# Eight pairs of hidden columns in two groups of seven products, with first writers of the output found at build time

## The chip, the cores and the metric

The kernel runs on one core of one Trainium2 chip. A core has five engines that run side by side and wait for one another through semaphores: TensorE (PE in the profile, its weight loads PEld), VectorE (DVE), ScalarE (ACT), GpSimd (POOL) and SyncE (SP), the last used here to issue DMAs. Matmuls write PSUM, of which the kernel has eight banks; everything else lies in SBUF or in DRAM. The metric is the device time of one execution in microseconds; before the change it is 1256.85 us, the median of three runs (1254.98 to 1257.09).

## What is computed

The reference sums the input, a long-convolution block and a feed-forward block (S = 2048 rows, D = 1024, F = 3584, float32):

```python
x = A_q
xn = _layernorm(x, axis=-1)
return x + _A_ref(xn, A_k, A_v, A_shift_k, A_ssm_k, A_ssm_D) + _B_ref(xn, B_w1, B_w2)
```

`_A_ref` filters `k` with four taps, multiplies by `v`, convolves each channel over the whole sequence (by FFT) with `ssm_k`, adds `kv * ssm_D`, and multiplies by `q`, here the normalised input. `_B_ref` is `silu(xn @ w1) @ w2`. The two matrix products are called GEMM1 and GEMM2 below.

## The kernel before

**Precision.** Every float32 operand of a large matmul is split into two float16 parts, and three matmuls (high x high, high x low, low x high) replace one. `split` makes the parts: ScalarE writes the high half (`a_act`, L360), VectorE the low half (`v_stt`, L352). Each split thus costs one ScalarE and one VectorE instruction over the same elements.

**Seven products.** GEMM1 takes the hidden columns in pairs of 128-column blocks (14 pairs, `NP`) and the rows in halves, and computes each 2 x 2 block product with seven products (P1 to P7, `PRODUCTS`) in place of eight. The price is sums and differences of blocks (S1 to S4, T1 to T4) ahead of the products. `units` runs the pairs for the first two row blocks (sp = 0) and then for the others (sp = 1); `evacuate` reads the PSUM banks, and `silu` follows.

**What becomes of the hidden activations.** For a plain pair `blocks` makes one 1024-wide split for each of the four row blocks and stores it in DRAM (`hs`). For a pair in `PAIRS` (8 to 11) `quad` makes, for each sp, three 1024-wide splits, one 512-wide split and four 512-wide sums, and stores seven tiles (`hsf`): the left operands of the seven products in GEMM2.

**GEMM2.** It runs in two halves of the output columns (h = 0 is the right half, `columns`), each half over 16 rows of 128 (t) and, for the plain pairs, five chunks of four hidden blocks (`NC` = 5), 12 matmuls a chunk (`steps2`, L1074 to L1076). Then `units2` runs pairs 8 to 11: eight tiles of seven products, each product 12 matmuls, each tile giving four 128 x 512 pieces of output (`evacuate2`). The W2 side is prepared by `norms_w2`: plain chunks by two 1024-wide splits each, the seven products by 28 narrow splits and 16 sums, in eight SBUF places that are handed on from GEMM1 (`W2PLACE`, `FPLACE`).

**The convolution** runs behind this in eight groups of 128 channels: `gate` (taps, times v), `signal_parts` (splits), `stage1` (matmuls with a DFT matrix), `to_spec` (PSUM to SBUF, ScalarE and VectorE), `forward`, `product` and `inverse` (butterflies and products on VectorE), `result_parts` (splits), `stage1_inv` (matmuls back), `gated` (times the normalised input, and out). A first transform may start only when the group before has finished its product, and its results may be written only once `result_parts` has taken the old ones (`taken`). Its PSUM tiles come from two banks (`ps_r`); `stage1_inv` has two others (`py_r`). During the plain part of GEMM2 both may also use a spare bank of the feed-forward ring `ff` (`spare`).

**Output.** Several contributions to each element of the output are summed in DRAM: one writer stores plainly (`L`, a DMA of the SP queue), the others accumulate (`G`, a DMA issued by GpSimd). Before the change it is fixed who writes first: `result` for h = 0, and the convolution's groups 0 to 3 for h = 1; all others wait for the flags `row` and `conv row` and accumulate. The last tile of GEMM2 waits for all of the convolution (`conv out`), reads back its piece (`hf<-out`), adds it and stores plainly.

**Order.** The program is written by generators, streams with a bias in microseconds. `Order.run` keeps a time for each engine and takes next the operation with the least start minus bias; of those that are ready at one time the largest bias goes first. Each engine then runs its instructions in the order so found. Quads have 0.1, evacuations 0.06, W2 0.05, the convolution 0.04 down to 0.02.

Of the kernel before, what the change touches and what calls it, by code (L numbers as in the profile page):

```python
# [53 lines left out]
PAIRS = (8, 9, 10, 11)  # L54
UNITS = [[*range(2, NP)], [NP - 1, 0, 1, *range(2, NP - 1)]]
NQ = len(PAIRS)
# [244 lines left out]
def h3_ffn_kernel(ctx, tc, x, kp, vs, fs, shift, dskip, w1, w2, cfwd, cinv, out):  # L301
# [77 lines left out]
    hsf = [{p[0]: dram.tile([4, P, NQ, 2, P], F16, name=f"hsf{p[0]}{b}") for p in PRODUCTS.values()} for b in range(2)]  # L379
# [449 lines left out]
    def quad(i, sp):  # L829

        def factors(names, hf, toks=()):
            n = len(names)
            yield hts.ready if n == 1 else hts.pairs
            ht, ttok = (hts.tile if n == 1 else hts.pair)([P, 4 * n, 2, P], F16, n)
            yield from split(ht[:, :, 0], ht[:, :, 1], hf, wsc[:, i, 2:3], toks)
            for f, name in enumerate(names):
                yield L(hsf[sp][name][:, :, PAIRS.index(i)].rearrange("q p h s -> p q (h s)"),
                        ht[:, 4 * f:4 * f + 4].rearrange("p q h s -> p q (h s)"))
# [12 lines left out]
        yield v_tt(z, x, z, SUB)  # L851
        add(factors(("S3", "S1"), flat[1], (ltok,)), 0.1)
        yield v_tt(x, v, x, SUB)
        ltok.set()
        yield v_tt(y, y, x, SUB)
        add(factors(("S2", "S4"), flat[0], (utok, flag["quads", sp])), 0.1)

    for sp in range(2):
        flag["quads", sp] = Token(NQ)

# [170 lines left out]
    def feed_forward():  # L1031
        first = [xo[0]["A11"], xo[0]["A12"]]
        r = [flag["rows", t] for t in range(4)]
        yield from plain_unit(0, 0, first, (r, r), 2)
        yield from plain_unit(1, 0, first, ((), ()))
        yield flag["x", 0, "A22"]
        lower = [second["A21"], xo[0]["A22"]]
        r = [(flag["x", 0, "A21"],), (flag["x", 0, "A22"],)]
        yield from plain_unit(0, 1, lower, r, free=True)
        yield from plain_unit(1, 1, lower, r, free=True)  # L1040
        second["tok"].set()
        flag["room", 0].set()
        yield from units()
        flag["gemm1"].set()
        for h in range(2):
            for ts in TOGETHER[h]:
                pos = {}
                for c in range(NC):
                    for t in ts:
                        if c == 0:  # L1050
                            yield ff.ready
                            pos[t] = ff.tile([P, W])
                        yield flag["h", h, t, c]
                        hx, htok = flag["h", h, t, c].what
                        yield flag["w2", h, c]
                        wc, wtok = w2c[h, c]
                        yield from steps2(pos[t][0], hx, wc, c == 0, c == NC - 1)
                        htok.set()
                        if t == NT - 1:
                            wtok.set()  # L1060
                        if c == NC - 1:
                            add(result(h, t, *pos[t]), EB)
        flag["last part"].set()
        yield from units2()


    TOGETHER = ([range(2)] + [(t,) for t in range(2, NT)],
                [(t,) for t in range(NT - 3)] + [range(NT - 3, NT)])

    def steps2(po, hx, wc, first, last, more=False):  # L1070
        for n in range(4):
            def mm(n=n):
# [3 lines left out]
                nc.tensor.matmul(po, hx[:, n, 1, :], wc[:, n, 0, :], start=False, stop=last and n == 3, **kw)  # L1076
# [15 lines left out]
    def units2():  # L1092

        def product2(n, u, o, first=False):
            yield flag["h2", u, n]
            hx, htok = flag["h2", u, n].what
            yield flag["w2f", n]
            wc, wtok = w2f[n]
            yield from steps2(o, hx, wc, first, True, not first)
# [7 lines left out]
        for u in range(len(tiles2)):  # L1107
# [3 lines left out]
            add(evacuate2(u, one, c, made, seen), EB)  # L1111
# [20 lines left out]

    def at(u, r, h):

        sp, q = tiles2[u]
        t = 4 * (2 * sp + r) + q
        return orr[t // T2, t % T2, :, h * W:(h + 1) * W]

    def evacuate2(u, one, c, made, seen):

        last = u == len(tiles2) - 1

        def copied(src, tok, to):
# [4 lines left out]
            yield G(to, o)  # L1148
# [12 lines left out]
        add(copied(*one, at(u, 0, 0)), EB)  # L1161
# [7 lines left out]
        yield G(at(u, 1, 1), d)  # L1169
# [9 lines left out]
        add(copied(two, k2, at(u, 0, 1)), EB)  # L1179
# [3 lines left out]
        yield L(at(u, 1, 0), a) if last else G(at(u, 1, 0), a)  # L1183
# [3 lines left out]
    for n in range(NT):  # L1187
        flag["conv row", n] = Token(NG // 2)

    def columns(h):  # L1190

        return slice((1 - h) * W, (2 - h) * W)

    def result(h, t, po, tok):
# [4 lines left out]
        to = orr[t // T2, t % T2, :, columns(h)]  # L1199
        if h == 0:  # L1200
            yield L(to, o)
            flag["row", t].set()
        else:
            yield flag["conv row", t]
            yield G(to, o)
        otok.set()

    def load_h():
        yield flag["factors"]
        for h in range(2):  # L1210
            for c, t in [(c, t) for ts in TOGETHER[h] for c in range(NC) for t in ts]:
# [4 lines left out]
        for u, n in uses2():  # L1216
            sp, q = tiles2[u]
            yield wo.ready
            flag["h2", u, n].what = o, _ = wo.tile([P, NQ, 2, P], F16)
            yield L(o, hsf[sp][PRODUCTS[n][0]][q])  # L1220
            flag["h2", u, n].set()
# [20 lines left out]
    def norms_w2():  # L1242
# [17 lines left out]
        add(load_w2(), 0.05)  # L1260
        for h in range(2):
            for c in range(NC):
                r = places[W2PLACE[h][c]]
                yield r.ready
                if (h, c) == (0, 0):
                    yield flag["x", 1, "A22"]
                wc, wtok = w2c[h, c] = r.tile([P, 4, 2, W], F16)
                flag["w2", h, c].n = 2
                for a in (0, 2):
                    i = PLAIN[4 * c + a] // 2  # L1270
                    raw, tok = yield from next_w2()
                    add(split(wc[:, a:a + 2, 0, :], wc[:, a:a + 2, 1, :], raw, tau[:, i:i + 1], (tok, flag["w2", h, c])), 0.05)
        yield places[FPLACE[0]].ready
        hold, ktok = places[FPLACE[0]].tile([P, NQ, W], F32)
        for k, (name, (_, of)) in enumerate(PRODUCTS.items()):
            r = places[FPLACE[k + 1]]
            yield r.ready
            wc, wtok = w2f[name] = r.tile([P, NQ, 2, W], F16)
            flag["w2f", name].n = NQ
            held = of in ("T2", "T3", "T4")  # L1280
            if held:
                if of != "T3":
                    yield flag["held", before]
                flag["held", of].n = NQ
                before = of
            for a, i in enumerate(PAIRS):
                raw, tok = yield from next_w2()
                src, toks = raw, (tok, flag["w2f", name])
                if held:
                    src, toks = hold[:, a], (flag["w2f", name], flag["held", of])  # L1290
# [16 lines left out]
        yield flag["held", "T4"]  # L1307
# [9 lines left out]
    def load_w2():  # L1317
        rings = ctxs["wraw"], ctxs["w2n"]
        for h, j in [(h, j) for h in range(2) for j in PLAIN[::2]]:
            yield lambda: any(r.pairs() for r in rings)  # L1320
            raw, tok = next(r for r in rings if r.pairs()).pair([P, 2, W])
            yield L(raw, w2r[:, j:j + 2, columns(h)])
            w2raw.append((raw, tok))
        for _, of in PRODUCTS.values():
            for i in PAIRS:
# [5 lines left out]


# [17 lines left out]
    def convolution(floor):  # L1350
# [141 lines left out]
        def stage1():  # L1492

            for g in range(NG):
# [4 lines left out]
                for t in TO:  # L1499
# [27 lines left out]

        def spare():
            return flag["gemm1"]() and not flag["last part"]() and len(ff.free()) > 1
# [189 lines left out]
        def gated(g, t, py, tok):  # L1719
# [13 lines left out]
            for b in range(2):  # L1733
                to = out4[b][:, :, t, g * P:(g + 1) * P]
                if g < NG // 2:
                    yield L(to, xg[:, b])
                else:
                    for n in rows[b]:
                        yield flag["row", n]
                    yield G(to, xg[:, b])  # L1740
                xtok.set()
                flag["conv out"].set()
                for n in rows[b]:
                    flag["conv row", n].set()
# [109 lines left out]
```

## Time and profile before

| | |
|---|---|
| time, median of three runs | 1256.85 us |
| profiled execution: time, span | 1258.14 us, 1256.4 us |
| granted TensorE clock, mean | 0.994 |
| busy of the span | PE 98%, PEld 48%, DVE 89%, ACT 63%, POOL 7% |
| first matmul of GEMM2, last matmul | 597.46 us, 1248.96 us |
| DMA | 279.83 MB, mean 223 GB/s |

The span runs from the first to the last instruction. Busy shares are means over stages that differ; the windows in the prediction give them for single stretches. In a timeline a row is start, duration, engine, line, operation, what is written and read, and in brackets the idle time ahead with what ended it. Durations of neighbouring instructions of an engine can overlap a little, so the prediction also uses the distance from start to start.

### The profile page before, as it was taken

What the parts mean: (1) busy time and instruction counts of PE and PEld (TensorE: products, weight loads), DVE (VectorE), ACT (ScalarE), POOL (GpSimd) and SP (SyncE); (2) the same over time, 40 slices, a digit from 0 to 9 for tenths busy, and PEclk for the clock granted to TensorE, in tenths of its full rate; (3) what the DMA queues carried; (4) which work ended last, traced back from release to release, by engine and by line L of the source; (5) the groups of instructions that cost most, each with busy time, mean ns of one, the idle gap of its engine ahead of it and who ended that gap; (6) DMA issues with size and microseconds to landing.
All of it is one profiled execution on the core that took longest, in us unless ns stands there. A gap on an engine that the chain in (4) does not pass through costs nothing. (4 is left out here: it accounts for less than half of the span.)

```text
span 1256.4 us, 17146 instructions
## 1 busy us (share of the span) xinstructions
PE 1232.6 (98%) x6034; PEld 597.5 (48%) x6034; DVE 1117.9 (89%) x1359; ACT 790.5 (63%) x1431; POOL 83.5 (7%) x93
## 2 busy tenths in 40 slices
PE   7999999999999999999999999999999999999996
PEld 6554444444444544444444544544544544454452
DVE  7999987997999789998999899799989889988970
ACT  7868888886588878568654643744653545563351
POOL 0000000000000000000000000000120030123132
PEclk8999999999999999999999999999999999999999
DMA  9276989989799899769984655688595497969765
GB/s 367 82 262 239 315 288 303 300 240 227 232 336 270 242 309 313 207 191 297 311 278 125 206 179 132 185 269 231 107 257 153 106 225 217 243 137 161 164 121 80
DMA packets 272662, 279.83 MB, mean 223 GB/s; under 512 B 73792, under 2 KB 192576, under 8 KB 271296
## 3 DMA queue, kind: packets, MB, share of 16 engines
q1 hardware_dynamic: 256848, 262.22, 67.9%
q0 software_dynamic: 15728, 16.52, 9.9%
q8 instruction: 47, 0.77, 0.3%
q14 instruction: 39, 0.32, 0.1%
HBM read 175.66 MB, written 88.34 MB: 210 GB/s over the span
## 5 line engine op out<-in xcount | busy, mean ns | idle before, releaser
L1074 PE MATMUL ff<-x,wo 128*128 128x512 f16 x864 | 327.9, 380 | 3.4 <-ACT hf L360 3.4
L1076 PE MATMUL ff<-x,wo 128*128 128x512 f16 x864 | 328.1, 380 | 0.0
L1075 PE MATMUL ff<-x,wo 128*128 128x512 f16 x864 | 327.9, 380 | 0.1
L946 PE MATMUL ff<-x,wo 128*128 128x512 f16 (+1 forms) x808 | 304.5, 377 | 6.2 <-ACT hf L360 3.0
L948 PE MATMUL ff<-x,wo 128*128 128x512 f16 (+1 forms) x808 | 304.8, 377 | 1.0 <-DVE wo L352 1.0
L947 PE MATMUL ff<-x,wo 128*128 128x512 f16 (+1 forms) x808 | 304.8, 377 | 0.0
L349 DVE TENSOR_TENSOR spec<-spec 128x512 f32<-128x512 f32 (+2 forms) x256 | 261.8, 1053 | 2.0
L1075 PEld LDWEIGHTS <-wo 128*128 128x128 f16 x864 | 84.6, 98 | 104.0 <-issue 4.7
L1076 PEld LDWEIGHTS <-wo 128*128 128x128 f16 x864 | 84.6, 98 | 102.6 <-issue 1.0
L1074 PEld LDWEIGHTS <-wo 128*128 128x128 f16 x864 | 85.5, 99 | 100.1 <-issue 0.6
L948 PEld LDWEIGHTS <-wo 128*128 128x128 f16 x808 | 79.6, 98 | 94.3 <-DVE wo L352 1.5
L947 PEld LDWEIGHTS <-wo 128*128 128x128 f16 x808 | 79.5, 98 | 93.8 <-issue 5.8
L946 PEld LDWEIGHTS <-wo 128*128 128x128 f16 x808 | 81.0, 100 | 90.2 <-ACT wo L360 1.7
L349 DVE TENSOR_TENSOR tmp<-spec 128x2048 f32<-128x2048 f32 (+1 forms) x48 | 92.7, 1933 | 0.9
L352 DVE SCALAR_TENSOR_TENSOR ht<-hf,wsc,ht 128x1024 f16<-128x1024 f32 (+1 forms) x56 | 67.4, 1203 | 7.5 <-ACT ht L360 7.2
L360 ACT ACTIVATE spec<-ps 128x512 f32<-128x512 f32 x92 | 53.2, 592 | 28.7 <-PE ps L1522 28.0
L352 DVE SCALAR_TENSOR_TENSOR wo<-raw,wsc,wo 128x512 f16<-128x512 f32 (+1 forms) x56 | 56.4, 1012 | 11.9 <-ACT wo L360 11.9
L346 POOL DMA_DIRECT2D out<-hf x47 | 45.8, 981 | 303.9 <-ACT hf L360 254.4
L360 ACT ACTIVATE hf<-ff,invc 128x512 f32<-128x512 f32 x32 | 21.9, 684 | 65.7 <-PE ff L1076 47.6
L360 ACT ACTIVATE ht<-hf,wsc 128x1024 f16<-128x1024 f32 (+1 forms) x56 | 60.8, 1085 | 3.4 <-DVE hf L349 2.1
L360 ACT ACTIVATE spec<-spec 128x1024 bf16<-128x1024 f32 x32 | 33.7, 1054 | 46.1 <-DVE spec L349 46.0
L349 DVE TENSOR_TENSOR spec<-tmp 128x512 f32<-128x512 f32 (+1 forms) x80 | 61.3, 792 | 0.7
(188 smaller groups left out, 1779.3 us busy)
## 6 DMA issues: line engine op xcount, KB each, us to landing
wo<-hs SPq DMA_DIRECT2D x160, 256.0 KB, 3.2
hs<-ht SPq DMA_DIRECT2D x80, 256.0 KB, 4.8
raw<-in_w SPq DMA_DIRECT2D x28, 512.0 KB, 5.9
wraw<-in_w SPq DMA_DIRECT2D x24, 512.0 KB, 5.4
w2n<-in_w SPq DMA_DIRECT2D x24, 512.0 KB, 6.1
out<-hf POOLq DMA_DIRECT2D x47, 256.0 KB, 4.5
kin<-in_kp SPq DMA_DIRECT2D x16, 704.0 KB, 5.1
xt<-in_x SPq DMA_DIRECT2D x16, 512.0 KB, 7.3
```

Of the source, the lines that this page charges most:

```text
L346: return Op("POOL", 1.1, 3.0, lambda: nc.gpsimd.dma_start(o, i, accum_op=ADD), [i], [o], m, 2.3 * n)
L349: return V(lambda: nc.vector.tensor_tensor(o, a, b, op=op), o, [a, b], **k)
L352: return V(lambda: nc.vector.scalar_tensor_tensor(o, a, s, b, op0=op0, op1=op1), o, [a, b] + ([] if isinstance(s, float) else [s]), **k)
L360: nc.scalar.activation(o, i, func, scale=scale, **kw)
L946: nc.tensor.matmul(o, w[:, 0, k], xf[:, :, k, 0], start=first and k == 0, stop=False, **kw)
L947: nc.tensor.matmul(o, w[:, 0, k], xf[:, :, k, 1], start=False, stop=False, **kw)
L948: nc.tensor.matmul(o, w[:, 1, k], xf[:, :, k, 0], start=False, stop=last and k == KH - 1, **kw)
L1074: nc.tensor.matmul(po, hx[:, n, 0, :], wc[:, n, 0, :], start=first and n == 0, stop=False, **kw)
L1075: nc.tensor.matmul(po, hx[:, n, 0, :], wc[:, n, 1, :], start=False, stop=False, **kw)
L1076: nc.tensor.matmul(po, hx[:, n, 1, :], wc[:, n, 0, :], start=False, stop=last and n == 3, **kw)
```

## The change

Eight pairs (4 to 11) instead of four go through GEMM2 in seven products, in two groups of four. The plain pairs shrink to six, three chunks. GEMM2's order becomes: plain rows of h = 0, the seven products of group 0 (both column halves), plain rows of h = 1, the seven products of group 1. The first half's rows now also end with a set of three rows together. The W2 preparation is cut into `plain_w2` and `seven_w2`, the latter for each group, with other places. Who writes an element of the output first is now recorded while the program is built (`first`, `written`, `put`): the first stores, the later ones accumulate, and a piece of which the convolution has written a part is cut in two. A first transform may use a bank of `py_r` once the group before has been taken from the spectrum (`bank_for`), and `spare` is now false during both runs of seven products.

```diff
-PAIRS = (8, 9, 10, 11)
+GROUPS = ((4, 5, 6, 7), (8, 9, 10, 11))
+PAIRS = sum(GROUPS, ())
...
-W2PLACE = [(2, 7, 6, 3, 4), (0, 1, 5, 2, 7)]
-FPLACE = (6, 3, 4, 0, 1, 5, 2, 7)
+W2PLACE = ((2, 7, 6), (3, 0, 1))
+FPLACE = ((3, 0, 1, 5, 4, 2, 7, 6), (5, 4, 2, 7, 6, 3, 0, 1))
...
         for h in range(2):
-            for ts in TOGETHER[h]:
+            for ts in TOGETHER:
...
-        flag["last part"].set()
-        yield from units2()
+            flag["seven", h].set()
+            yield from units2(h)
+            flag["plain", h + 1].set()
+
+    TOGETHER = [range(2)] + [(t,) for t in range(2, NT - 3)] + [range(NT - 3, NT)]
...
     flag["conv out"] = Token(NG * 4 * 2)
-    for n in range(NT):
-        flag["conv row", n] = Token(NG // 2)
+    first = {}
+
+    def written(places_in, to, o):
+
+        new = [q not in first for q in places_in]
+        assert len(set(new)) == 1
+        if new[0]:
+            for q in places_in:
+                first[q] = Token()
+            yield L(to, o)
+            for q in places_in:
+                first[q].set()
+            return
+        for q in places_in:
+            yield first[q]
+        yield G(to, o)
...
-        to = orr[t // T2, t % T2, :, columns(h)]
-        if h == 0:
-            yield L(to, o)
-            flag["row", t].set()
-        else:
-            yield flag["conv row", t]
-            yield G(to, o)
+        yield from put(t, h, o)
         otok.set()
+
+    def put(t, h, o):
+        groups = range(h * NG // 2, (h + 1) * NG // 2)
+        there = sum((t, g) in first for g in groups)
+        for part in (groups[there:], groups[:there]):
+            if part:
+                a, b = part[0] * P, (part[-1] + 1) * P
+                yield from written([(t, g) for g in part], orr[t // T2, t % T2, :, a:b], o[:, a - h * W:b - h * W])
...
         for h in range(2):
+            yield from plain_w2(h)
+            yield flag["quads", 1]
+            yield from seven_w2(h)
...
-                                yield lambda: ps_r.ready() or spare()
-                                ps, tok = (ps_r if ps_r.ready() else ff).tile([P, 2, 2 * P])
+                                yield lambda: bank_for(g, t) is not None
+                                ps, tok = bank_for(g, t).tile([P, 2, 2 * P])
...
+        def bank_for(g, t):
+
+            if ps_r.ready():
+                return ps_r
+            if g > 0 and py_r.ready() and flag["taken", g - 1, t]():
+                return py_r
+            return ff if spare() else None
+
         def spare():
-            return flag["gemm1"]() and not flag["last part"]() and len(ff.free()) > 1
+            if not flag["gemm1"]() or len(ff.free()) < 2:
+                return False
+            return not flag["seven", 0]() or flag["plain", 1]() and not flag["seven", 1]()
...
-                to = out4[b][:, :, t, g * P:(g + 1) * P]
-                if g < NG // 2:
-                    yield L(to, xg[:, b])
+                cs = slice(g * P, (g + 1) * P)
+                a, c = rows[b]
+                if ((a, g) in first) == ((c, g) in first):
+                    yield from written([(a, g), (c, g)], out4[b][:, :, t, cs], xg[:, b])
                 else:
-                    for n in rows[b]:
-                        yield flag["row", n]
-                    yield G(to, xg[:, b])
+                    for i, n in enumerate(rows[b]):
+                        yield from written([(n, g)], out4[b][:, i, t, cs], xg[:, b, i])
```

More of the change, by code (lines that the diff above doesn't have):

```diff
@@ L1110, in units2 @@
             c = ff.tile([P, W])
-            add(evacuate2(u, one, c, made, seen), EB)
+            add(evacuate2(k, u, one, c, made, seen), EB)
             yield from product2("P7", u, c[0], True)
@@ L1160, in evacuate2 @@
         yield made["P2"]
-        add(copied(*one, at(u, 0, 0)), EB)
+        add(copied(*one, row_of(u, 0), 0), EB)
         yield ws_r.ready
@@ L1178, in evacuate2 @@
         yield made["P3"]
-        add(copied(two, k2, at(u, 0, 1)), EB)
+        add(copied(two, k2, row_of(u, 0), 1), EB)
         yield made["P4"]
@@ L1215, in load_h @@
                 flag["h", h, t, c].set()
[L1216 to L1221, printed above, removed]
+            for u, n in uses2():
+                sp, q = tiles2[u]
+                yield wo.ready
+                flag["h2", h, u, n].what = o, _ = wo.tile([P, 4, 2, P], F16)
+                yield L(o, hsf[sp, h][PRODUCTS[n][0]][q])
+                flag["h2", h, u, n].set()
     def squares_w2():
```

163 lines of the change are left out of this document (89 added, 74 removed).

## The prediction, made before the changed kernel ran

> **What bounds the kernel now.** I read the page first, then the busy time by stretch, then single operations.
>
> ```profile
> span 1256.4 us, 17146 instructions
> PE 1232.6 (98%) x6034; PEld 597.5 (48%) x6034; DVE 1117.9 (89%) x1359; ACT 790.5 (63%) x1431; POOL 83.5 (7%) x93
> ...
> L1074 PE MATMUL ff<-x,wo 128*128 128x512 f16 x864 | 327.9, 380 | 3.4 <-ACT hf L360 3.4
> ```
>
> TensorE sets the end. Whether its 98% is a full array shows in the spacing of matmuls in the timeline of TensorE:
>
> ```profile
> 1141.47 0.38 PE L1074 MATMUL ff<-x,wo 128*128 128x512 f16 x1
> ...
> 1153.99 0.38 PE L1075 MATMUL ff<-x,wo 128*128 128x512 f16 x1
> ```
>
> These two are 58 matmuls apart: 12.52 / 58 = 0.216 us each, without a gap. A matmul that goes away therefore gives 0.216 us, as long as nothing else ends later. VectorE at 89% is the one that could. The windows (us, then busy time of PE, PEld, DVE, ACT, POOL, granted clock, DMA share, GB/s) show two stretches that are each one channel group of the convolution and little else, two hand-overs from one group to the next, and the whole of GEMM2 up to the convolution's end:
>
> ```profile
> 711.50:808.70 97.20, 97.20 (x478) 46.70 (x477) 90.20 (x98) 47.80 (x101) 0.00 (x0) 1.00 0.59 168
> 919.90:1018.00 98.10, 98.10 (x482) 47.09 (x481) 90.24 (x98) 48.34 (x102) 15.88 (x16) 1.00 0.69 168
> ...
> 420.00:451.00 31.00, 31.00 (x163) 15.77 (x161) 20.54 (x26) 27.10 (x53) 0.76 (x1) 1.00 0.90 256
> ...
> 686.00:711.50 25.50, 25.50 (x143) 13.89 (x142) 18.57 (x24) 20.06 (x41) 0.76 (x1) 1.00 0.58 169
> ...
> 604.00:1222.50 618.50, 617.78 (x3020) 295.52 (x3019) 567.73 (x614) 312.07 (x623) 71.05 (x74) 1.00 0.72 189
> ```
>
> One group needs 90.2 us of VectorE and takes 97 to 98. The convolution goes as fast as VectorE lets it, all the way to 1222.5, and leaves VectorE only 618.5 - 567.7 = 50.8 us of idle time in GEMM2, nearly all of it in hand-overs, where ScalarE is busy 20.06 of 25.5 us (27.10 of 31.0 in GEMM1). What then stands between the convolution's end and the kernel's end is in the timeline (VectorE, GpSimd, the SP queue):
>
> ```profile
> 1221.86 0.69 DVE L349 TENSOR_TENSOR ht<-py,ht 128x512 f32<-128x512 f32 x1 [1.05 <-ACT py L360]
> ...
> 1230.07 1.11 POOL L346 DMA_DIRECT2D out<-ht  x1 [3.27 <-issue]
> ...
> 1245.45 0.33 SPq L336 DMA_DIRECT2D hf<-out  x1
> ...
> 1248.84 0.69 DVE L349 TENSOR_TENSOR hf<-hf 128x512 f32<-128x512 f32 x1 [4.11 <-DMA hf<-out]
> ...
> out<-ht POOLq DMA_DIRECT2D x16, 128.0 KB, 4.4
> ```
>
> The last accumulate of the convolution starts at 1230.07 and lands about 4.4 us later, at 1234.5. The last tile of GEMM2 reads its finished output back at 1245.45. So the convolution has 1245.45 - 1234.5 = **11.0 us of slack**, no more; a convolution later by x ends the kernel at 1256.4 - 11.0 + x = 1245.4 + x, if TensorE is done by then.
>
> **The change part by part.** *TensorE.* Plain chunks go from five to three per half: 2 halves x 16 rows x 2 chunks x 12 matmuls = 768 fewer. The second group adds 8 tiles x 7 products x 12 = 672. Net 96 fewer x 0.216 = **20.7 us less**. Weights for P5, P3 and P4 of a group go into places that the last three plain rows set free, as before; that hand-over exists already and L1074, the first matmul of each step, waited 3.4 us in all, so I cost it at 0. If the weights come late instead, P5 is first.
>
> *VectorE.* Durations by shape, and the pitch at which such instructions follow one another:
>
> ```profile
> 718.40 1.28 DVE L352 SCALAR_TENSOR_TENSOR acc<-kin,taps,acc 128x1024 f32<-128x1024 f32 x1
> 719.60 1.22 DVE L349 TENSOR_TENSOR spec<-spec 128x1024 f32<-128x1024 f32 x1
> ...
> 740.58 0.69 DVE L349 TENSOR_TENSOR acc<-acc,lo 128x512 f32<-128x512 f32 x1
> 741.19 0.69 DVE L349 TENSOR_TENSOR spec<-spec 128x512 f32<-128x512 f32 x1
> ...
> 1065.76 0.74 DVE L352 SCALAR_TENSOR_TENSOR x<-wraw,tau,x 128x512 f16<-128x512 f32 x1
> 1066.42 0.75 DVE L352 SCALAR_TENSOR_TENSOR x<-w2n,tau,x 128x512 f16<-128x512 f32 x1
> ```
>
> Pitches: 1.20 us for the low half of a 1024-wide split, 0.60 for a 512-wide sum, 0.66 for the low half of a 512-wide split. Pairs 4 to 7 lose 16 plain blocks (16 x 1.20 = 19.2) and get 8 quads of three wide splits, one narrow split and four sums (3.6 + 0.66 + 2.4 = 6.66; 8 x 6.66 = 53.3): +34.1. Their W2 loses 8 wide splits (9.6) and gets 28 narrow splits and 16 sums (18.5 + 9.6 = 28.1): +18.5. The eight added tiles of seven products have two 512-wide steps each: 16 x 0.66 = +10.6. Together **+63.2 us of VectorE**. The planner takes, of the streams that are ready, the one with the larger bias; quads have 0.1, W2 0.05, evacuation 0.06, the convolution 0.02 to 0.04, so it is the convolution that is pushed back.
>
> *What of the 63.2 us falls into idle time.* The new quads come four units ahead of pair 8's, whose first splits are the two ht<-x rows; a unit is 84 matmuls, 18.1 us, so about 72 us ahead: around 133 and 436.
>
> ```profile
> 205.12 1.28 DVE L352 SCALAR_TENSOR_TENSOR ht<-x,wsc,ht 128x1024 f16<-128x1024 f32 x1 [0.38 <-ACT ht L360]
> ...
> 508.86 1.28 DVE L352 SCALAR_TENSOR_TENSOR ht<-x,wsc,ht 128x1024 f16<-128x1024 f32 x1
> ...
> 130.00:210.00 80.00, 80.00 (x378) 36.98 (x377) 68.27 (x91) 67.73 (x103) 0.94 (x1) 1.00 0.93 316
> ...
> 434.00:508.00 74.00, 74.00 (x353) 34.46 (x352) 66.89 (x79) 57.33 (x110) 0.76 (x1) 1.00 0.96 296
> ...
> DVE spec L349 <- ACT spec L360: 24.5, 13, 5.4
> ...
> DVE tmp L349 <- ACT spec L360: 6.4, 11, 1.2
> ```
>
> (The last two rows are waits after 600: us in total, times, longest.) In the first (17 us of quads) 80 - 68.27 = 11.7 us are idle, ahead of the convolution's first transform: between 0 and 11.7 absorbed, I take 9. In the second (17 us) 7.1 us, part of it a hand-over that ScalarE fills: 0 to 7.1, I take 4. In GEMM2 the 29.1 us (W2 and tiles) come evenly, and hand-overs of about 25 us in each 100 to 125 are a fifth of the time: a fifth, 6 (0 to 29).
>
> *More banks for the first transform* (`bank_for`, `spare`). The profile has no run with four banks. What they can shorten are VectorE's waits for ScalarE's copy of a first transform: 24.5 + 6.4 = 31 us after 600 in the rows above, and by the two quoted hand-overs up to 31.0 - 27.10 = 3.9 and 25.5 - 20.06 = 5.4 us each, the part in which ScalarE is not busy: eight of them, at most about 37. Below nothing it goes too: the ff banks are now shut to it in both runs of seven products, not only the last. I take half, 19 (from -8 to 37).
>
> Absorbed or won: 9 + 4 + 6 + 19 = 38, so x = 63.2 - 38 = 25.2.
>
> *ScalarE* gets as many high halves plus five copies for each of the eight tiles; with 63% busy it has room outside the hand-overs, and inside them it is why I do not take more above. *DMA:* 24 more 256 KB writes of activations in GEMM1 (112 + 48 against 56 + 80), eight fewer reads in GEMM2; TensorE waits for none of this now; with that cover gone 6.3 MB at 316 GB/s would be 20 us. *Output:* eight tiles add 32 stores; about 40 more accumulates go through GpSimd, 7% busy, and a first writer now goes through SP, in order with the loads; nothing there.
>
> **Sum.** 1245.4 + 25.2 = 1270.6 in the profiled execution's span. Its own time is 1258.14, 1.7 above its span, but the median of the runs shown, 1256.85, is 0.45 above it; on that scale **1271 us**. TensorE would be done at 1249 - 20.7 = 1228 and waits for nothing: its saving is not seen.
>
> **Rivals.** *A, the saving shows.* If the new banks and the idle time absorb more than 63.2 - 8.5 = 54.7 us, the convolution slips by less than 8.5 and the kernel ends before 1254.3; with all absorbed and 9.7 won besides TensorE stays last: 1256.4 - 20.7 + 0.45 = 1236. For it: VectorE is idle 50.8 us in GEMM2 and 18.8 in the two stretches of the quads, and waits on ScalarE are what the new banks aim at. Against it: hand-overs are four fifths ScalarE work, which grows. *B, nothing is absorbed:* x from 48 to 63, 1294 to 1309; the hand-overs stay as they are, and only the 13 to 15 us of the early quads may go under.
>
> *C, GpSimd and VectorE block each other.* 40 more accumulates of 0.86 to 2.5 us, if a sum on VectorE stood still for each, would be 34 us or more on top of x: 1305.
>
> ```profile
> L346 POOL DMA_DIRECT2D out<-hf x47: 859/862/2497, 852.5 to 1250.6; - x47
> ...
> 1143.00:1209.00 66.00, 66.00 (x309) 30.08 (x308) 65.07 (x66) 19.62 (x34) 12.95 (x15) 1.00 0.77 162
> ...
> L349 DVE TENSOR_TENSOR spec<-tmp x8: 681/688/693, 1168.8 to 1189.9; 128x512 f32<-128x512 f32 x8
> ```
>
> (The first and last row give counts with the shortest, median and longest duration in ns.) Against it: from 1143 to 1209, with 15 such instructions on GpSimd, VectorE's sums last 681 to 693 ns, none is stretched; it is some of GpSimd's that are. The Trainium skill's page "SBUF — State Buffer" says under "Who interferes with whom" that a VectorE instruction with two SBUF inputs and a GpSimd one that reads SBUF lock each other out for a whole instruction. By that rule either engine may be the one that waits; the trace has GpSimd as the loser (2497 ns at most against a median of 862), so the rule adds nothing to VectorE's sum.
>
> **How the numbers follow.** The forecast (convolution last, 1258 to 1292, by itself most likely 1262 to 1285) 0.66; A (1236 to 1254) 0.22; between these, 0.04; B 0.05; C 0.03. About 0.2%, 2.5 us, is what a measurement of this kernel can tell from no change: faster 0.22, same 0.05, slower 0.73. The range 1241 to 1292 leaves out the lower end of A (some 0.07) and B with C.
>
> **What would show it.** Right: TensorE's last GEMM2 matmul but those of the last tile about 20 us earlier, VectorE above 92% busy, the last convolution sum (ht<-py) at 1240 to 1255, the read-back of out waiting for it. Each step: 96 fewer matmuls; 32 fewer wide splits from hf or raw weights; hand-overs shorter by 2 to 3 us with transforms in py banks. Wrong: a last convolution sum before 1230, hand-overs below 20 us, or TensorE waiting in the middle for weights (ff<-x,wo after a split of x).

## The result and the profile after

| | before | after |
|---|---|---|
| median | 1256.7 us (1254.98 to 1257.09) | 1273.11 us (1270.66 to 1274.6) |
| ratio, 95% interval | | 1.0128 [1.0106, 1.0149] |
| profiled run: time, span | 1258.14, 1256.4 us | 1271.68, 1269.9 us |
| granted TensorE clock | 0.994 | 0.986 |
| matmuls | 6034 | 5938 |
| convolution's last sum starts | 1221.86 us | 1259.18 us |
| last matmul of GEMM2 starts | 1248.96 us | 1239.86 us |

The change makes the kernel 16.4 us slower, by the medians. The forecast was 1271 us. The page of the changed kernel, the lines that answer to those of before (busy us, share of the span, instructions):

```profile
span 1269.9 us, 17329 instructions
PE 1217.7 (96%) x5938; PEld 589.3 (46%) x5938; DVE 1179.5 (93%) x1459; ACT 831.2 (65%) x1507; POOL 116.6 (9%) x130
...
L1075 PE MATMUL ff<-x,wo 128*128 128x512 f16 x832 | 315.6, 379 | 6.1 <-ACT hf L361 5.1
```

VectorE has 1179.5 - 1117.9 = 61.6 us more to do; 63.2 were worked out. The matmuls are 96 fewer. The first matmuls of a step of GEMM2 (L1075) wait 6.1 us in all, 5.1 of them for ScalarE's evacuation and none to speak of for weights. The last rows of TensorE's GEMM2, of the SP queue, of VectorE and of GpSimd in the timeline of the changed kernel (start, duration, engine, line, what is written and read):

```profile
1239.86 0.38 PE L1077 MATMUL ff<-x,wo 128*128 128x512 f16 x1
...
1236.81 0.34 SPq L337 DMA_DIRECT2D hf<-out  x1
...
1259.18 0.69 DVE L350 TENSOR_TENSOR ht<-py,ht 128x512 f32<-128x512 f32 x1 [1.05 <-ACT py L361]
1259.79 0.68 DVE L350 TENSOR_TENSOR hf<-hf 128x512 f32<-128x512 f32 x1
...
1261.71 2.19 POOL L347 DMA_DIRECT2D out<-ht  x2 [0.30 <-issue]
1263.41 1.41 POOL L347 DMA_DIRECT2D out<-hf  x1
```

The convolution now ends last: TensorE's GEMM2 has been over for 19 us when its last sum starts. The way in which it sets the end differs from the prediction. The read-back of the last tile (`hf<-out`, the SP row) goes out 22 us *ahead* of the convolution's last sum, so it doesn't wait for it; the columns that it reads belong to groups 0 to 3. The flag `conv out`, which the last tile is said to wait for, only orders the program while it is built: it places these instructions behind those of the convolution in each engine's queue. So what comes late is the sum that uses the read-back (`hf<-hf`): it stands on VectorE behind the convolution's last instruction, whose end it follows at once. The last tile's accumulate (`out<-hf`) stands in the same way on GpSimd behind the convolution's own accumulates (`out<-ht`): ScalarE has its data ready at 1261.20, GpSimd issues it at 1263.41. From the end of the last sum (1259.9) to the end of the span it is 10 us.

VectorE's time is compared best at fixed places of the convolution: the starts of the last products of its first, second and third group. The second lies in GEMM1 in both kernels, the third 64 us into GEMM2 before the change and 98 us into it after. The windows between these places, first of before, then of after (busy time of PE, PEld, DVE, ACT, POOL, granted clock, DMA share, GB/s):

```profile
0.00:383.43 383.43, 373.76 (x1864) 188.56 (x1865) 345.67 (x509) 301.93 (x503) 2.40 (x8) 0.99 0.83 265
383.43:516.18 132.75, 132.75 (x645) 62.94 (x643) 118.91 (x140) 106.31 (x197) 0.76 (x1) 1.00 0.93 279
...
0.00:661.65 661.65, 649.02 (x3185) 318.33 (x3186) 603.69 (x797) 505.94 (x867) 3.91 (x10) 0.99 0.85 267
661.65:1222.50 560.85, 560.13 (x2751) 269.24 (x2750) 510.56 (x559) 280.54 (x559) 71.05 (x74) 1.00 0.71 179
```

```profile
0.00:408.08 408.08, 395.44 (x1958) 198.12 (x1959) 371.23 (x543) 319.49 (x532) 2.41 (x8) 0.99 0.85 269
408.08:556.18 148.10, 146.59 (x708) 69.16 (x707) 141.71 (x172) 113.77 (x202) 0.76 (x1) 1.00 0.89 278
...
0.00:694.29 694.29, 672.29 (x3280) 328.28 (x3281) 643.84 (x861) 522.33 (x896) 3.92 (x10) 0.99 0.86 269
694.29:1259.80 565.51, 545.45 (x2660) 261.06 (x2657) 534.25 (x597) 308.16 (x610) 108.00 (x116) 0.99 0.81 194
```

At the second place, inside GEMM1, VectorE has done 48.4 us more (371.23 + 141.71 against 345.67 + 118.91) and the convolution is already 40.0 us late, so idle time took up only 8.4. At the third it has done 643.84 - 603.69 = 40.2 us more and the place comes 32.6 us later: 7.5 absorbed. From there to the convolution's end it does 23.7 us more, and the stretch is only 565.51 - 560.85 = 4.7 us longer: 19.0 are absorbed. The loss was made in GEMM1.

### The profile page after: what moved, and what is told of

It reads as the page before. It is cut to its first block, busy times and chain, and to the rows that moved or that the text cites. A ratio compares the mean times of both kernels' runs of the same rounds, so it can differ in the third digit from the quotient of the medians.

```text
span 1269.9 us, 17329 instructions
## 1 busy us (share of the span) xinstructions
PE 1217.7 (96%) x5938; PEld 589.3 (46%) x5938; DVE 1179.5 (93%) x1459; ACT 831.2 (65%) x1507; POOL 116.6 (9%) x130
## 3 DMA queue, kind: packets, MB, share of 16 engines
q0 software_dynamic: 21568, 24.92, 14.2%
## 4 chain that ended last, share of the span: by engine, by line
PE 67%; DVE 16%; issue 7%; DMA 5%; ACT 3%; POOL 2%; SPq 0%; POOLq 0%; DVEq 0%; ACTq 0%
PE ff L951 11%; PE ff L949 11%; PE ff L950 11%; PE ff L1075 9%; PE ff L1077 8%; PE ff L1076 8%; DVE spec L350 5%; DVE tmp L350 2%; POOL out L347 2%; DVE spec L353 1%; PE ps L1564 1%; DVE ht L353 1%; PE ps L1566 1%; PE ps L1565 1%; DVE acc L353 1%
## 5 line engine op out<-in xcount | busy, mean ns | idle before, releaser
L1075 PE MATMUL ff<-x,wo 128*128 128x512 f16 x832 | 315.6, 379 | 6.1 <-ACT hf L361 5.1
L949 PE MATMUL ff<-x,wo 128*128 128x512 f16 (+1 forms) x808 | 304.9, 377 | 13.6 <-DVE hf L350 9.5
L1076 PE MATMUL ff<-x,wo 128*128 128x512 f16 x832 | 315.4, 379 | 0.0
L1077 PE MATMUL ff<-x,wo 128*128 128x512 f16 x832 | 315.4, 379 | 0.0
L1076 PEld LDWEIGHTS <-wo 128*128 128x128 f16 x832 | 81.4, 98 | 102.8 <-issue 8.3
L1077 PEld LDWEIGHTS <-wo 128*128 128x128 f16 x832 | 81.4, 98 | 98.4 <-issue 0.3
L950 PEld LDWEIGHTS <-wo 128*128 128x128 f16 x808 | 79.5, 98 | 101.7 <-issue 14.7
L1075 PEld LDWEIGHTS <-wo 128*128 128x128 f16 x832 | 82.3, 99 | 95.5 <-issue 0.3
L951 PEld LDWEIGHTS <-wo 128*128 128x128 f16 x808 | 79.5, 98 | 98.9 <-DVE wo L353 6.0
L949 PEld LDWEIGHTS <-wo 128*128 128x128 f16 x808 | 81.0, 100 | 90.3 <-ACT wo L361 1.7
L347 POOL DMA_DIRECT2D out<-hf x79 | 71.8, 913 | 341.7 <-ACT hf L361 210.0
L361 ACT ACTIVATE hf<-ff,invc 128x512 f32<-128x512 f32 x64 | 43.3, 681 | 57.8 <-PE ff L1077 41.7
L347 POOL DMA_DIRECT2D kf<-in_dskip x8 | 7.5, 937 | 734.3 <-DMA kf<-in_fs 241.9
L353 DVE SCALAR_TENSOR_TENSOR ht<-hf,wsc,ht 128x1024 f16<-128x1024 f32 (+1 forms) x56 | 63.1, 1127 | 7.9 <-ACT ht L361 7.4
L353 DVE SCALAR_TENSOR_TENSOR acc<-kin,taps,acc 128x1024 f32<-128x1024 f32 x48 | 61.3, 1278 | 6.6 <-ACT acc L361 6.5
```

The lines of the kernel that those rows point to most:

```text
L347: return Op("POOL", 1.1, 3.0, lambda: nc.gpsimd.dma_start(o, i, accum_op=ADD), [i], [o], m, 2.3 * n)
L353: return V(lambda: nc.vector.scalar_tensor_tensor(o, a, s, b, op0=op0, op1=op1), o, [a, b] + ([] if isinstance(s, float) else [s]), **k)
L361: nc.scalar.activation(o, i, func, scale=scale, **kw)
L949: nc.tensor.matmul(o, w[:, 0, k], xf[:, :, k, 0], start=first and k == 0, stop=False, **kw)
L950: nc.tensor.matmul(o, w[:, 0, k], xf[:, :, k, 1], start=False, stop=False, **kw)
L951: nc.tensor.matmul(o, w[:, 1, k], xf[:, :, k, 0], start=False, stop=last and k == KH - 1, **kw)
```

## The experiments

Theory V is the prediction's: the convolution on VectorE ends last, and the end follows it. Its rivals: TensorE's new waits hold the kernel by themselves (P), the place of the groups or the order on VectorE counts (Q), GpSimd and VectorE block each other (C). Ratios are to the kernel before.

### How much slack the convolution had

```diff
 # after the product 128x2048 of each part n, in the kernel before
+                if n in (0,):        # e1; n in (0, 1) in e2
+                    yield v_tt(run(tmp, 0, 16), steps_of(xx, 0, (2 * P, 4), (0, 4)), run(k, 0, 4, (4 * P, 2), (0, 2)), MUL)
```

> The kernel before, with the widest VectorE product of each convolution group (2048 elements, 2.2 us) done once more: +17.6 us of VectorE in the convolution, nothing else. Theory V (VectorE carries the convolution, whose end has some 24 us of slack in the kernel before, as the last read-back needs groups 0 to 3 alone): 1255 to 1260, no change. The prediction's slack of 11 us: 1263. Rival P (the change is slower because TensorE waits in the middle, the convolution's lateness has no price): 1257.

> The same product done once more in two of its four places: +35.2 us of VectorE. Theory V with 24 us of slack: 1257 + 35 - 24 = 1268, between 1264 and 1272. The prediction's slack of 11 us: 1281. Rival P: 1257.

Measured: 1255.99 us, ratio 1.0002 [0.9988, 1.0016], for 17.3 us more on VectorE (1135.2 against 1117.9), and 1262.79 us, ratio 1.0052 [1.0034, 1.0070], for 35.2 us more. VectorE at the end, with one product more, then with two:

```profile
1232.16 0.69 DVE L349 TENSOR_TENSOR ht<-py,ht 128x512 f32<-128x512 f32 x1 [1.26 <-ACT py L360]
...
1246.63 0.69 DVE L349 TENSOR_TENSOR hf<-hf 128x512 f32<-128x512 f32 x1 [5.15 <-DMA hf<-out]
```

```profile
1247.77 0.69 DVE L349 TENSOR_TENSOR ht<-py,ht 128x512 f32<-128x512 f32 x1 [1.05 <-ACT py L360]
1248.38 0.68 DVE L349 TENSOR_TENSOR hf<-hf 128x512 f32<-128x512 f32 x1
```

In the first the convolution ends 10 us later than before and nothing is lost: the sum of the last tile still waits for its data. That is still within 11.0 us of slack, so this run alone decides nothing. In the second it ends 1247.77 - 1221.86 = 25.9 us later, and the sum follows it without a gap. There and in the changed kernel the span ends 10.0 us after the convolution. By that the kernel before could have finished its convolution 1256.4 - 10.0 - 1222.5 = 23.9 us later. The profiled execution of e2 was the fastest of its four; by the medians e2 loses 6.8 us, which leaves 25.9 - 6.8 = 19.1 us of slack. Either way the prediction's 11.0 us, by which e2 would have lost 14.9, is wrong. The expected 1264 to 1272 was missed by 1.2 us.

### The kernels without the last two groups

```diff
-            for g in range(NG):
+            for g in range(6):
```

(in every loop of the convolution; `flag["conv out"]` counts six groups)

> The kernel before without the convolution's groups 6 and 7 (their part of the output is left out): 180 us of VectorE less, and 2 x 15.6 = 31 us of TensorE less. TensorE ends last in every theory: 1222 to 1230.

> The changed kernel without the convolution's groups 6 and 7. Theory V: with VectorE relieved the 96 matmuls show, 20.7 us below the run before it less what TensorE's new waits cost: 1204 to 1214. Rival P: not below the run before it, 1224 or more.

Measured: 1221.17 us, ratio 0.9718 [0.9700, 0.9737], and 1223.53 us, ratio 0.9737 [0.9717, 0.9757]. With a convolution that is done long before TensorE in both, the changed kernel should have been 20.7 us faster by the matmuls that it lacks; by the medians it is not faster at all, in the profiled executions by 2.5 us. The pages, before and after with six groups:

```profile
span 1220.8 us, 16188 instructions
PE 1198.5 (98%) x5834; PEld 576.9 (47%) x5834; DVE 940.2 (77%) x1167; ACT 703.5 (58%) x1241; POOL 63.8 (5%) x75
```

```profile
span 1218.3 us, 16376 instructions
PE 1182.3 (97%) x5738; PEld 568.4 (47%) x5738; DVE 1003.3 (82%) x1267; ACT 748.5 (61%) x1317; POOL 96.8 (8%) x112
```

TensorE is busy 16.2 us less and idle 1218.3 - 1182.3 = 36.0 instead of 22.3 us. Its waits, in the second (us in total, times, longest):

```profile
PE ff L949 <- DVE hf L350: 9.5, 2, 6.8
PE ff L951 <- DVE wo L353: 4.6, 3, 3.0
```

So P is a second floor under the changed kernel, and the expected 1204 to 1214 was missed: GEMM1 waits on VectorE for sums of its tiles and for weight splits (1.8 and 1.1 us in the run before it), which eats most of what fewer matmuls give. In the full kernels the same shows in the stretch from 130 to 604, first the one before, then the changed one:

```profile
PE ff L946 <- DVE hf L349: 1.8, 1, 1.8
```

```profile
PE ff L949 <- DVE hf L350: 9.5, 2, 6.8
PE ff L951 <- DVE wo L353: 3.0, 1, 3.0
```

### Fewer pairs, and pairs in another place

```diff
-GROUPS = ((4, 5, 6, 7), (8, 9, 10, 11))
+GROUPS = ((6, 7), (8, 9, 10, 11))          # e5, with places for four chunks
+GROUPS = ((6, 7, 8, 9), (10, 11, 12, 13))  # e6
```

> The changed kernel with six pairs in seven products, groups (6, 7) and (8 to 11): against the kernel before 48 matmuls less (10.4 us) and 36.9 us more of VectorE. If the convolution's end alone decides (theory V), it slips by about 22 us, less than its slack, and TensorE ends last: 1246 to 1250. If TensorE's new waits in GEMM1 come with it (theory P, in the changed kernel they eat what the 96 matmuls save, as the runs with six convolution groups show), half of them: 1252 to 1257. With the prediction's slack of 11 us: 1267.

> The changed kernel with groups (6 to 9) and (10 to 13): the same work, but the added quads come after the layer norm's second rows instead of among them, so that the convolution's first transform should start near 320 us instead of 348. If only the sum of VectorE's work counts: 1270 to 1276. If its place counts: 1258 to 1267.

Measured: 1298.43 us, ratio 1.0336 [1.0320, 1.0352], and 1280.55 us, ratio 1.0196 [1.0179, 1.0214]. Both missed what either theory expected. In the first, a group of two has half the matmuls per product, but each tile still needs the same evacuations, and TensorE starves. Its stretch in the windows, then its longest wait from 680 to 920:

```profile
837.00:919.00 82.00, 58.00 (x227) 24.08 (x227) 76.46 (x83) 40.18 (x82) 17.52 (x20) 0.86 0.87 206
...
PE ff L1075 <- ACT hf L361: 14.1, 5, 6.3
```

TensorE is idle 24 of 82 us there at a granted clock of 0.86; the convolution's last sum starts at 1266.22, 30 us ahead of the end, so this kernel is bound by TensorE. It says nothing on VectorE's sum of work, for which it was meant. In the second the convolution is last (1267.19) and the groups are equal in work to the changed kernel's. Its first wide product starts at 380.58 us, against 379.87 in the changed kernel, so the start of the convolution, which this run was meant to move, did not move; why two pairs later costs 7 us more is not settled.

### What the extra work costs in GEMM1 and in GEMM2

```diff
+            if i in GROUPS[0]:            # e7: no low halves of group 0's quads
+                yield a_act(ht[:, :, 0], hf, AF.Copy, wsc[:, i, 2:3])
+                for t in toks:
+                    t.set()
+            else:
+                yield from split(ht[:, :, 0], ht[:, :, 1], hf, wsc[:, i, 2:3], toks)
...
+                    if g > 0:             # e9: no W2 sums of group 0, and no VectorE step of its tiles
+                        yield v_tt(src, raw, b12, SUB)
```

> The changed kernel without the low halves of group 0's quads (their VectorE splits in GEMM1 are left out, 24 wide and 8 narrow: 34 us of VectorE less). Theory V: the convolution ends 25 to 34 us earlier, TensorE ends last; theory P: its waits in GEMM1 go with that VectorE work, so 1236 to 1244. If the waits stay (they come from ScalarE or from places): 1254 to 1258.

> The changed kernel without the sums of group 0's W2 operands and without the two VectorE steps in each of its tiles (20 us of VectorE less, all in GEMM2). Theory V alone: 1273 - 18 = 1253 to 1256. With theory P, whose waits lie in GEMM1 and stay: not below 1257, 1257 to 1261. If neither holds (GpSimd's accumulates end last): 1270 or more.

Measured: 1250.77 us, ratio 0.9956 [0.9940, 0.9973], and 1266.16 us, ratio 1.0083 [1.0060, 1.0105]. The windows around the third place of the convolution, of e7, and the one behind it of e9:

```profile
0.00:660.11 660.11, 646.56 (x3167) 316.46 (x3168) 609.12 (x829) 520.26 (x890) 3.91 (x10) 0.99 0.89 277
660.11:1238.20 578.09, 568.04 (x2773) 271.73 (x2771) 535.52 (x597) 313.32 (x617) 104.75 (x113) 1.00 0.83 196
```

```profile
693.84:1253.00 559.16, 545.56 (x2662) 261.14 (x2660) 520.38 (x573) 310.11 (x610) 107.89 (x116) 0.99 0.83 197
```

In e7 VectorE has 643.84 - 609.12 = 34.7 us less to do up to that place, and the place comes 694.29 - 660.11 = 34.2 us earlier: at that place each microsecond of VectorE in GEMM1 has moved the convolution by one, none of the quads' splits was hidden. TensorE's waits for VectorE's sums in GEMM1 went with them, from 9.5 to 0.4 us, so the run doesn't part V from P. From there on the same busy time takes 12.6 us longer, and at the end 21.6 us of the gain are left. In e9 13.9 us less after that place shorten the stretch by 6.4: in GEMM2 less than half of such work is on the path. Both times missed what was expected, e7 between the 1236 to 1244 and the 1254 to 1258, e9 between the 1257 to 1261 and the 1270. In e7 the convolution ends 21.6 us earlier, where theory V had 25 to 34.

### The banks for the first transform

```diff
 # e8: the changed kernel without
-            if g > 0 and py_r.ready() and flag["taken", g - 1, t]():
-                return py_r
 # e14: the kernel before with
+                                yield lambda: bank_for(g, t) is not None
+                                ps, tok = bank_for(g, t).tile([P, 2, 2 * P])
```

> The changed kernel, but the first transform of a group may no longer take a free bank of the inverse transforms (py); all else as changed. Theory V (the time follows the convolution's end, which follows VectorE's work and its waits at the hand-overs): the prediction put the banks at 19 us, so the convolution would end at about 1278 and the kernel at 1288 to 1292. In the two traces VectorE's waits for ScalarE's copy of a first transform fell from 24.5 to 7.9 us and the hand-overs after 600 by 0 to 8 us each; by these the banks are worth 10 to 17 us and the time is 1281 to 1289. Rival: ScalarE sets the hand-overs, whatever the banks: the time stays within 1268 to 1276.

> The kernel before with one part of the change alone: the first transform of a group may take a free bank of the inverse transforms (py). VectorE's and TensorE's work is as before. Theory S (the convolution of the kernel before has about 24 us of slack and TensorE's last tiles set its end): the convolution's last sum comes earlier, at 1197 to 1215 in place of 1221.9, and the time stays within 0.4 per cent of before, 1252 to 1261. Rival (the prediction's slack of 11 us: the end follows the convolution closely): the time falls by as much as the convolution leaves free of TensorE's own work, to under 1250.

Measured: 1297.7 us, ratio 1.0327 [1.0307, 1.0347], and 1257.84 us, ratio 1.0014 [1.0004, 1.0025]. VectorE's last sums, without the banks in the changed kernel, then with them in the kernel before:

```profile
1285.86 0.69 DVE L350 TENSOR_TENSOR ht<-py,ht 128x512 f32<-128x512 f32 x1 [1.05 <-ACT py L361]
```

```profile
1216.75 0.69 DVE L349 TENSOR_TENSOR ht<-py,ht 128x512 f32<-128x512 f32 x1 [1.05 <-ACT py L360]
...
1246.84 0.69 DVE L349 TENSOR_TENSOR hf<-hf 128x512 f32<-128x512 f32 x1 [5.65 <-DMA hf<-out]
```

In the changed kernel the banks are worth 26.7 us of the convolution's end and 24.6 us of time, more than the 19 that were predicted and more than the 10 to 17 read from the waits. In the kernel before the same banks bring the convolution's end only 5.1 us earlier, to 1216.75, just short of the expected 1197 to 1215, and no time is won: the difference is 0.14%, and the sum of the last tile waits for its data as ever. That fits theory S. Where the two values part shows at the last product of the fifth, sixth and eighth group, of the changed kernel and then of the same without the banks:

```profile
913.60 2.29 DVE L350 TENSOR_TENSOR tmp<-spec 128x2048 f32<-128x2048 f32 x1
...
1023.52 2.29 DVE L350 TENSOR_TENSOR tmp<-spec 128x2048 f32<-128x2048 f32 x1
...
1222.76 2.29 DVE L350 TENSOR_TENSOR tmp<-spec 128x2048 f32<-128x2048 f32 x1
```

```profile
927.28 2.29 DVE L350 TENSOR_TENSOR tmp<-spec 128x2048 f32<-128x2048 f32 x1
...
1036.73 2.29 DVE L350 TENSOR_TENSOR tmp<-spec 128x2048 f32<-128x2048 f32 x1
...
1250.62 2.29 DVE L350 TENSOR_TENSOR tmp<-spec 128x2048 f32<-128x2048 f32 x1
```

Without the banks the fifth group is 13.7 us behind, the sixth 13.2, the eighth 27.9; nothing is lost on the way to the sixth. In the changed kernel the loads of activations for seven products go out between 708.54 and 885.47 and again from 1031.35 on: in these stretches the ff banks are shut to the first transform, and between them, where the sixth group changes over, they are open. This suggests that the banks mostly repay what shutting the ff banks takes away, and are worth little where those stay open, as in the kernel before. Shutting them alone was not tried.

### The order on VectorE, and sums on GpSimd

```diff
-                add(quad(i, sp), 0.1)
+                add(quad(i, sp), 0.045)   # e10, and so the two adds of factors
...
-        yield v_tt(v, z, v, ADD)
+        yield p_tt(v, z, v, ADD)          # e13: nc.gpsimd.tensor_tensor, 64 sums of the quads and 32 of W2
```

> The changed kernel with the bias of the quads' streams at 0.045 in place of 0.1: below the splits of W2 (0.05) and the evacuations (0.06), still above the convolution (0.02 to 0.04). Theory Q (TensorE's new waits in GEMM1, 9.5 us for sums and 4.1 us for splits on VectorE, come from the quads being taken ahead of what TensorE waits for): these waits shrink to under 4 us and the time falls by 4 to 10 us, to 1263 to 1269. Rival V alone (only VectorE's sum of work counts, in whatever order): the convolution's last sum stays within 3 us of 1259.2 and the time within 1270 to 1275, whatever TensorE waits for in GEMM1.

> The changed kernel with the sums of the quads (64) and of the W2 operands of GEMM2 (32) on GpSimd in place of VectorE; the splits stay. VectorE loses 96 sums x 0.60 = 57.6 us and stands near 1122 us, about where it was before the change. Theory V: the convolution ends 35 to 55 us earlier, at 1205 to 1225, TensorE ends last and the kernel takes 1238 to 1252, less than both. Rival C (GpSimd and VectorE block each other): VectorE's sums beside GpSimd's are stretched above 0.69 us, VectorE's busy time falls by much less than 57.6 us, and the time is 1265 or more. Rival L: no block, but the quads and operands come later since a sum takes longer on GpSimd (its duration is in no row so far), and TensorE waits for them: VectorE's busy time falls by 57 us and TensorE's waits for x and wo grow, 1252 to 1270.

Measured: 1294.52 us, ratio 1.0300 [1.0278, 1.0322], and 1325.73 us, ratio 1.0543 [1.0517, 1.0568]. Theory Q had the sign wrong. With the quads behind the evacuations TensorE waits more for tiles, not less (e10, from 130 to 604):

```profile
PE ff L949 <- ACT hf L361: 16.2, 5, 5.1
```

In the changed kernel this row has 2.5 us, and the wait for VectorE's sums stays nearly as it was (8.9 us after 9.5). VectorE's work is the same (1179.7 us), but the convolution's last sum starts at 1280.97. V alone, "in whatever order", falls with it. A quad that is late keeps the buffers of its tiles, which would explain it; that was not shown.

The sums on GpSimd are the worst of all. The first of GpSimd's rows (count, busy us and mean ns), then VectorE's of the changed kernel and of e13:

```profile
L358 POOL TENSOR_TENSOR x<-x 128x512 f32<-128x512 f32 x16 | 34.7, 2170 | 1.3
```

```profile
L350 DVE TENSOR_TENSOR spec<-spec 128x1024 f32<-128x1024 f32 x104 | 124.7, 1218 | 0.4
L353 DVE SCALAR_TENSOR_TENSOR x<-x,tau,x 128x512 f16<-128x512 f32 x24 | 17.5, 744 | 0.0
L350 DVE TENSOR_TENSOR hf<-ff,hf 128x512 f32<-128x512 f32 x52 | 35.6, 684 | 3.9 <-PE ff L951 2.7 <-ACT hf L361 1.1
```

```profile
L350 DVE TENSOR_TENSOR spec<-spec 128x1024 f32<-128x1024 f32 x104 | 137.7, 1342 | 0.4
L353 DVE SCALAR_TENSOR_TENSOR x<-x,tau,x 128x512 f16<-128x512 f32 x24 | 23.6, 993 | 3.2 <-ACT x L365 3.2
L350 DVE TENSOR_TENSOR hf<-ff,hf 128x512 f32<-128x512 f32 x52 | 35.5, 682 | 5.6 <-PE ff L955 4.5 <-ACT hf L365 1.1
```

Without the 96 sums VectorE would be busy 1179.5 - 57.6 = 1121.9 us; it is busy 1206.2, so 84 us of stretching replace 58 us of sums. Rows with both operands in SBUF are longer; the row that reads ff, which is in PSUM, is not. Rival C is real for work that GpSimd does itself. It isn't the whole price: VectorE is busy 26.7 us longer than in the changed kernel, the time is 52.6 us longer, and TensorE's waits ahead of the first matmuls of GEMM1's steps grow from 13.6 to 35.8 us, as rival L has it for sums that come later. How much each costs was not parted. In the changed kernel GpSimd only issues DMAs, 130 instructions against 93 before, and there VectorE's rows have the durations of before (1218 ns for the 128x1024 sum, 1219 before): C took no part in the result.

No kernel here that does all the work beats the one before; e7 is faster by leaving work out.

## Why the prediction came out right

**The direction and the main mechanism** hold: the convolution on VectorE ends last, and the kernel with it. VectorE's added work was right within 1.6 us and the matmuls exactly. (The sign of "32 fewer wide splits" doesn't follow from the prediction's own working, and the rows have 16: 8 fewer from `hf`, 8 fewer from raw weights.)

**Two of its terms were wrong and offset each other.** The delay x of the convolution was predicted as 25.2 us; it is 1259.18 - 1221.86 = 37.3. The slack was predicted as 11.0 us; it is 23.9 by the profiled executions, 19.1 by the medians of e2. So 37.3 - 23.9 = 13.4 us later, in place of 25.2 - 11.0 = 14.2; the spans differ by 13.5. The good forecast of the size is luck: one term was 12 us too small and the other 13 us too small, and they are subtracted.

**The step of the slack failed by its mechanism.** "The last tile of GEMM2 reads its finished output back at 1245.45" was taken for the point that waits for the convolution. It doesn't wait: in the changed kernel it goes out 22 us before the convolution's last sum. The convolution reaches the end through the order of instructions, on VectorE (the rows of e1 and e2) and on GpSimd, where the last tile's accumulate stands behind the convolution's. Which of the two queues would hold the end alone was not tried.

**The step of the early quads failed**: 9 + 4 us of absorption in GEMM1. By the windows, up to the first group's last product VectorE does 25.6 us more and is 24.7 us late, so 0.9 us were absorbed in place of 9; from there to the second group's it does 22.8 more in a stretch that is 15.4 longer, so 7.4 in place of 4. The first idle stretch was seen rightly and then given back, as these windows show (first 210 to 320 before the change, then both stretches of the changed kernel):

```profile
210.00:320.00 110.00, 110.00 (x525) 51.53 (x524) 96.31 (x127) 86.37 (x142) 0.00 (x0) 1.00 0.93 255
...
130.00:210.00 80.00, 80.00 (x378) 36.95 (x377) 79.44 (x107) 70.11 (x107) 0.00 (x0) 1.00 0.91 304
210.00:320.00 110.00, 106.87 (x503) 49.59 (x501) 88.80 (x118) 83.45 (x136) 0.95 (x1) 0.98 0.97 275
```

From 130 to 210 VectorE's idle time falls from 11.7 to 0.6 us. In the next 110 us it rises from 13.7 to 21.2, and TensorE stands still for 3 us. VectorE's longest waits there are for ScalarE: those for the copy of the first transform grow from 3.7 to 8.4 us.

**GEMM2's terms came out in sum, not one by one.** Of 29.1 us, 6 and 19 were to be absorbed, which leaves 4.1. Behind the third place 23.7 us were added and 19.0 absorbed, which leaves 4.7. Over the whole convolution 7.5 + 19.0 = 26.5 us were absorbed, where the prediction had 38: that is nearly all by which x was too small. The banks measured 24.6 us, but in the kernel before they move the convolution by only 5.1 us, so the 19 isn't a price that holds by itself: it was taken as a gain over before, and seems to be mostly the return of a loss that the prediction named ("the ff banks are now shut to it") and priced only as the lower end of its range.

**"TensorE would be done at 1228 and waits for nothing" was wrong.** GEMM2's last matmul is 9.1 us earlier, not 20.7. New waits of TensorE took the rest, as with six groups. Rival A's 1236 us was therefore out of reach: even with the convolution out of the way, the changed kernel would by estimate end some 7.4 us (the distance in the profile before, 1256.4 - 1248.96) after 1239.86, at 1247. The pair with six groups leaves it less than that, 2.5 us in the profiled executions and nothing by the medians.

**What would show it**: the last sum was expected at 1240 to 1255 and came at 1259.18; VectorE is above 92% busy, as said. TensorE's last matmul is not 20 us earlier, and the read-back doesn't wait for the convolution.

## What to carry to other kernels

Before a change that takes matmuls away and pays in VectorE's time, find where the idle time of VectorE lies: time next to a stretch that is full already is not there to be used, and the delay travels through every later group. Slack is to be read from the instructions that stand behind the late one in the queues of its engines, not from the nearest DMA in time; adding a known amount of work to the kernel before measures it, once it delays the late part by more than the slack. And fewer matmuls are worth their time only where nothing that TensorE waits for becomes later.

## What the hardware showed besides

**GpSimd's own sums stretch VectorE.** A 128x512 sum took GpSimd 1.6 to 2.5 us in the mean of its groups, against 0.69 on VectorE, and splits from SBUF on VectorE went from 744 to 993 ns in the mean. The Trainium skill's page "SBUF — State Buffer" says under "Who interferes with whom" that a VectorE instruction with two SBUF inputs contends with a GpSimd one that reads SBUF, and one with at most one SBUF input doesn't, outside the modes in which VectorE uses both of its ports. The trace of e13 agrees on both: 993 ns for the split, 682 for the sum with a PSUM input.

**A long wait of TensorE cost more than its length.** The changed kernel around its longest wait in GEMM1, and a window behind it (duration, PE busy with its count, granted clock, DMA share, GB/s):

```profile
591.32 0.59 PE L949 MATMUL ff<-x,wo 128*128 128x512 f16 x1 [6.83 <-DVE hf L350]
591.70 0.63 PE L950 MATMUL ff<-x,wo 128*128 128x512 f16 x1
...
596.39 0.63 PE L1075 MATMUL ff<-x,wo 128*128 128x512 f16 x1
...
591.30:595.00 3.70, 3.68 (x9) 0.50 1.20 279
```

From 591.70 to 596.39 eleven matmuls follow at (596.39 - 591.70) / 11 = 0.426 us each, about twice the 0.216 of the full clock, at a granted clock of 0.50: 2.3 us more are lost behind a wait of 6.83. In the same trace the matmuls behind a wait of 3.04 us (at 273.33) follow one another at 0.43 us too, five of them, and those behind a wait of 2.92 us (at 912.29) at 0.22.
